# A recurrent attention block and a soft mixture of experts in one kernel: all tasks emitted in another order

## Chip, cores and metric

The kernel runs on one core of a Trainium2 chip. The metric is the device time of one execution in microseconds (us); the figure for the kernel before is the median of three runs. Engines: PE multiplies and transposes (TensorE), DVE, ACT and POOL work elementwise (VectorE, ScalarE, GpSimd), SP issues plain transfers; 16 DMA engines move data.

## What is computed

First a linear recurrence over 768 time steps for 4 batches and 8 heads of width 48, then a soft mixture of 8 experts with 4 slots each over the 3072 rows that come out of it:

```python
for t in range(S):
    kt, vt, rt = (k[:, :, t], v[:, :, t], r[:, :, t])
    cur = np.einsum('bhd,bhe->bhde', u[None] * kt, vt)
    y[:, :, t] = np.einsum('bhd,bhde->bhe', rt, state + cur)
    state = w[None, :, :, None] * state + np.einsum('bhd,bhe->bhde', kt, vt)
...
logits = x @ phi
d = softmax(logits, axis=0); c = softmax(logits, axis=1)
slot_input = (d.T @ x).reshape(E, S_per_e, D)
for e in range(E):
    slot_out[e] = np.maximum(slot_input[e] @ w1[e], 0.0) @ w2[e]
return c @ slot_out
```

(The two softmax lines are shortened; x is y with the heads side by side, 384 wide.) Inputs are float32: r, k, v of 4.7 MB each, w1 and w2 of 12.6 MB each. The output is 3072 x 384 in float32, 4.7 MB.

## The kernel before

**Data.** Time is cut into chunks of 128 steps and blocks of 256. Two batches are handled side by side, so there are 6 blocks U (0 to 5) and 12 steps n of the recurrence (0 to 11; n = 2U and 2U + 1 belong to block U; the state starts anew at n = 6). Loads bring float32 from memory and turn it into bf16 on the way; such loads are issued by POOL. For each block there are six of them, the two halves (batches) of k, r and v in this order: `raw` tile 6U + 2 x which + half, called raw 0 to raw 35 below. Raw 0 alone is loaded by SP and turned by ACT, so raw n is the n-th load on POOL as long as they are in this order. Weights come as one load for each expert (768 KB as bf16): w1 into `w1_all`, w2 into `raw` tiles that are no longer needed; w2 of expert 7 in three parts.

**Work.** `turned` transposes raw tiles on PE (line 419, 16 to a piece), and DVE or ACT writes them to SBUF with the decay factors (lines 430, 427); for blocks after the first, POOL multiplies k by r for each step (line 443, "the product of step n"). `step(n)` transposes k and v back (457), multiplies k by r under a mask (484, 489), forms the sum of k times v and adds the old state (515, 519; the result is `Ssp`), copies it (ACT, 526) and scales it by the decay on POOL (529): this is Z(n, hh), the state behind step n, for the two halves hh of the heads. The next step needs both halves on PE. From the product of line 443 PE and DVE make `dv` (503, 535). The output of a step (552, 557, 559) goes to `x_all`, is transposed (581) and gives the logits (600). `combine` and `dispatch` are the two softmaxes (616 to 652 and 704 to 773; the E sum of line 620 and Le of 636 are on POOL). `first_layer` and `second_layer` are the experts (842 to 905), `output` the last product and the stores (926 to 935, 8 DMAs on SP).

**Order.** Each piece is registered with `task(...)`: engine, assumed duration, what it reads and writes, which buffers it uses. `Plan.order` gives each task a time; when the list `SEQ` is given, it takes the tasks in that order and only computes times. For a load it assumes a queue, and through `lag` that a load waits for the landing of the load `lag` places before it. `Plan.emit` then emits all tasks in that order; where it thinks PE idle at the beginning or after the last step, it puts in filling matmuls (`idle`, line 912). So in this kernel the assumed durations and lags change nothing but the fillers (and which buffer of a ring a task gets); the list is the order.

Every instruction is emitted through `O`, which pins it behind the last instruction emitted on its engine:

```python
def O(ins):
    return tc.keep_in_program_order(ins)
```

A scheduler behind that orders each engine's instructions as pins and data allow. One operation breaks the chain: `pool.affine_select` emits two instructions, a register move (the fill value) and the select. The select is pinned behind the register move, which is itself pinned to nothing. A select, and what is emitted behind it on POOL, is therefore free to move ahead of what was emitted before it. There are four selects of this kind outside the beginning, which build the small matrix `sumI` (lines 679 to 682, tasks 105 to 108 in the numbering of the kernel before):

```python
for i in range(4):
    task(10, "POOL", 0.28, lambda i=i: O(pool.affine_select(
        out=sumI[:], in_=sumI[:], compare_op=ALU.not_equal, fill=1.0, base=-32 * i, ...
```

In the built program each load on POOL takes one of eight semaphores in turn, and waits before its issue for the load that had the semaphore last, the one eight places ahead on POOL.

Of the kernel before, what the change touches and what calls it, by code (L numbers as in the profile page):

```python
# [12 lines left out]
class Plan:  # L13
# [40 lines left out]
    def order(self):  # L54
# [4 lines left out]
            for d in x[4]:  # L59
                after.setdefault(d, []).append(i)  # L60
        ready = [i for i in range(len(tasks)) if not wait[i]]
        t, queue, out = 0.0, 0.0, []
        count, block = 67, -10.0
        while ready:
            best = None
            if self.seq:
                i = self.seq[len(out)]
                assert not wait[i]
                eng, use = tasks[i][1], tasks[i][5]
                at = max(since[i], free.get(eng, 0.0))  # L70
                need = [k[0] for k in use if k not in self.slot]
                for k in need:
                    got = sorted(f for f in self.pools[k] if f is not None)
                    at = max(at, got[need.count(k) - 1])
                best = (at, 0.0, i, at)
            for i in () if self.seq else ready:
                prio, eng, _, _, _, use, _, _ = tasks[i]
                at = max(since[i], free.get(eng, 0.0), t)
                more, hold = self.tune.get(i, (0.0, 0.0))
                if best is not None and at + hold > best[0]:  # L80
                    continue
                need = {}
                for k in use:
                    if k not in self.slot:
                        need[k[0]] = need.get(k[0], 0) + 1
                for k, m in need.items():
                    got = sorted(f for f in self.pools[k] if f is not None)
                    at = max(at, got[m - 1]) if len(got) >= m else 1e9
                key = (at + hold, prio + more, i, at)
                if best is None or key < best:  # L90
                    best = key
            assert best[0] < 1e8, [tasks[i][:3] for i in sorted(ready)[:20]]
            _, _, i, t = best
            prio, eng, dur, fn, deps, use, dma, n = tasks[i]
            for k in use:
                if k not in self.slot:
                    p = self.pools[k[0]]
                    s = min((x for x in range(len(p)) if p[x] is not None), key=lambda x: p[x])
                    self.slot[k] = s
                    p[s] = None  # L100
            if eng == "PE":
                if (count + 2 * n) // 256 > count // 256:

                    part = dur * (256 - count % 256) / (2 * n)
                    begin = max(t + part, block + 6.0)
                    dur += begin - t - part
                    block = begin
                count += 2 * n
            free[eng] = t + dur
            e = t + dur  # L110
            if dma is not None:
                queue = max(queue, t + dur + 1.3) + dma
                e = queue + 1.6
            end[i] = e
            ready.remove(i)
            for d in after.get(i, ()):
                wait[d] -= 1
                since[d] = max(since[d], e + (SAME[eng] if eng == tasks[d][1] and dma is None else LAT[eng]))
                if not wait[d]:
                    ready.append(d)  # L120
            for k in use:
                left[k].discard(i)
                if not left[k]:
                    self.pools[k[0]][self.slot[k]] = max(end[j] + LAT[tasks[j][1]] for j in self.users[k])
            out.append((t, len(out), i))
# [4 lines left out]
    def emit(self, where, fill, took=0.22):  # L130
# [9 lines left out]
            self.tasks[i][3]()  # L140

TUNE = {}
SEQ = [89, 58, 4, 57, 9, 52, 2, 62, 102, 0, 5, 10, 53, 54, 6, 12, 11, 13, 63, 104, 1, 65, 66, 3, 14, 75, 47, 59, 46,
# [27 lines left out]

# [3 lines left out]
def kernel(  # L175
# [32 lines left out]
    f32 = mybir.dt.float32  # L208
# [6 lines left out]
    def O(ins):  # L215
        return tc.keep_in_program_order(ins)

    pe, dve, act, pool, sp = nc.tensor, nc.vector, nc.scalar, nc.gpsimd, nc.sync
# [4 lines left out]
    def sb(name, shape, dt):  # L223
        return big.tile(shape, dt, name=name)
# [56 lines left out]
    ident = sb("ident", [128, 128], bf)  # L281
    by_head = sb("by_head", [128, 128], bf)
    by_time = sb("by_time", [128, 128], bf)
    ones_f = sb("ones_f", [32, 128], f32)
    mask = sb("mask", [128, 128], f32)
    biasP = sb("biasP", [128, 1], f32)
    wuT = sb("wuT", [128, 16], f32)
# [7 lines left out]
    def load(U, which):  # L295
        src = (k, r, v)[which]
        p, n = divmod(U, nU)
        for x in range(2):
# [6 lines left out]
                task(-95, "ACT", 0.83, lambda: O(act.copy(raw_of(0, 0, 0), st)), r=["st"], w=[("raw", 0)])  # L305
            else:
                task(-100 + U, "POOL", 0.54, lambda ap=ap, x=x: O(pool.dma_start(out=raw_of(which, U, x), in_=ap)), w=[("raw", i)],  # L307
                     dma=0.955, lag=7)

    O(act.preload_act_table_set("natural_log_exp_and_others"))  # L310
    both = lambda m: m[:, None, :].to_broadcast([H, 2, D])
# [30 lines left out]
        out=er, in0=Rf, scalar1=-float(C), scalar2=None, op0=ALU.add)), r=["Rf"], w=["er"])  # L342
    for a, b, val in ((0, 128, -200.0), (0, D, 0.0), (64, 64 + D, 0.0)):
        task(-160, "DVE", 0.1, lambda a=a, b=b, val=val: O(dve.memset(biasP[a:b, :], val)), w=["biasP"])
    task(-150, "DVE", 0.1, lambda: O(dve.memset(ones_f[:], 1.0)), w=["ones_f"])
    task(-150, "DVE", 0.1, lambda: O(dve.memset(ucol[:], 0.0)), w=["ucol"])
    for i in range(2):
        task(-150, "DVE", 0.25, lambda i=i: O(dve.memset(Le_t[i][:], 0.0)), w=["Le0"])
# [468 lines left out]
    w2_first = {}  # L817

    def load_w(e, second, part=0):
        lag = 7 if not second and e < 3 else 5  # L820
        if not second:
            task(-50 + e, "POOL", 0.57, lambda: O(pool.dma_start(
                out=w1_all[:, e, :, :], in_=moe_w1[e].rearrange("(p mo) f -> p mo f", p=128))), w=[("w1", e)], dma=3.7, lag=lag)
# [166 lines left out]
```

## Time and profile before

| | |
|---|---|
| three runs | 121.63, 118.66, 119.14 us; median 119.14 |
| the profiled execution | 120.11 us, its span (first to last instruction) 118.3 us |
| PE busy | 99.1 us (84%) |
| DVE, ACT, POOL busy | 92.1, 78.8, 72.5 us |
| software DMA queue (all POOL loads) | 19.47 MB written, 85.7% of 16 engines' time |
| mean granted clock of PE | 0.959 |

Times inside the profile count from the first instruction. The profile has the busy share of each engine in 40 slices and, on demand, in stages; the chain of waits, followed back from the last instruction; the instructions of an engine in order of time, with the idle time ahead of each and what ended it in brackets; and the DMA issues with the median time from issue to landing. A DMA share over 1 comes from packets that overlap.

### The profile page before, as it was taken

To read this page: it belongs to the slowest core of one execution; us is meant where nothing else is said; L and a number is where in the kernel's file an instruction comes from. 1 tells how busy PE (TensorE), PEld (TensorE's weight loads), DVE (VectorE), ACT (ScalarE), POOL (GpSimd) and SP (SyncE) were. 2 spreads that over 40 slices of the span, in tenths; PEclk is the share of its full clock that TensorE was granted. 3 is DMA by queue.
4 is the path that set the end of the run, shared out by engine and by line. 5 is a ranking of instruction groups with operands and counts; after the bars stand their busy time and mean duration, and the time that the engine had idled before them with its cause. 6 is when DMAs were issued, how large, how long until landed. Compare 5 with 4: busy or idle time off the path is not lost.

```text
span 118.3 us, 4300 instructions
## 1 busy us (share of the span) xinstructions
PE 99.1 (84%) x1849; PEld 73.1 (62%) x1849; DVE 92.1 (78%) x156; ACT 78.8 (67%) x161; POOL 72.5 (61%) x112
## 2 busy tenths in 40 slices
PE   4999992999999999999959899989999997656100
PEld 0365781888787788887848687868664554445000
DVE  5999899469999999999979999999976540277400
ACT  4483894299675899899739688978984631265400
POOL 6967768979979988999187878895622300000000
PEclk9999998599999999999999999999999999999955
DMA  2999999999999999999999999999999995069993
GB/s 35 237 189 197 209 206 208 205 208 207 206 200 186 168 208 210 220 211 218 213 220 209 222 209 216 217 212 219 208 219 214 209 206 91 9 224 404 417 415 137
DMA packets 9283, 24.91 MB, mean 210 GB/s; under 512 B 1200, under 2 KB 6192, under 8 KB 9264
## 3 DMA queue, kind: packets, MB, share of 16 engines
q0 software_dynamic: 7632, 19.47, 85.7%
q1 hardware_dynamic: 1584, 5.16, 11.5%
q8 instruction: 14, 0.23, 0.7%
q14 instruction: 5, 0.04, 0.1%
q10 hardware_dynamic: 48, 0.01, 0.0%
HBM read 39.38 MB, written 4.72 MB: 373 GB/s over the span
## 4 chain that ended last, share of the span: by engine, by line
PE 55%; DMA 21%; POOL 5%; issue 4%; DVE 4%; ACT 3%; DVEq 0%; POOLq 0%
PE T L419 12%; DMA raw<-in_moe_w_dram 11%; DMA raw<-in_k_dram 7%; PE T L457 7%; PE Ab L484 6%; PE Y L552 5%; PE T L581 4%; DMA raw<-in_r_dram 4%; PE Y L559 3%; PE Y L515 3%; DVE arena L933 3%; PE Y L557 3%; PE Y L519 3%; POOL raw L307 2%; PE Sb L503 2%
## 5 line engine op out<-in xcount | busy, mean ns | idle before, releaser
L430 DVE TENSOR_TENSOR arena<-T,tab 128x1024 bf16<-128x1024 bf16 x24 | 28.6, 1210 | 3.6 <-PE T L419 3.6
L489 DVE TENSOR_TENSOR arena<-Ab,mask 128x1024 bf16<-128x1024 f32 x24 | 29.2, 1216 | 0.6 <-PE Ab L484 0.5
L419 PE MATMUL T<-by_head,raw 128*48 128x128 bf16 x576 | 22.2, 223 | 0.4 <-issue 0.4
L443 POOL TENSOR_TENSOR arena<-arena 128x1024 bf16<-128x1024 bf16 x10 | 21.4, 2142 | 0.8 <-DVE arena L430 0.8
L529 POOL TENSOR_TENSOR Z<-Ss,wCm 128x384 bf16<-128x384 f32 x20 | 16.6, 833 | 7.6 <-ACT Ss L526 7.5
L419 PEld LDWEIGHTS <-raw 128*48 128x48 bf16 x576 | 17.1, 104 | 4.7 <-issue 2.3
L427 ACT COPY arena<-T 128x1024 bf16<-128x1024 bf16 x12 | 12.1, 1019 | 3.4 <-PE T L419 3.2
L526 ACT COPY Ss<-Y 128x384 f32<-128x384 f32 x20 | 9.6, 491 | 6.3 <-PE Y L519 6.1
L566 ACT CAST x_all<-Y 128x384 bf16<-128x384 f32 x23 | 11.2, 486 | 3.8 <-PE Y L559 3.5
L457 PE MATMUL T<-ident,arena 112*128 112x112 bf16 x176 | 12.4, 217 | 0.0
L535 DVE TENSOR_TENSOR dv<-vn,Sb 128x768 bf16<-128x768 bf16 x12 | 11.3, 943 | 0.4 <-PE Sb L503 0.4
L457 PEld LDWEIGHTS <-arena 112*128 112x128 bf16 x176 | 9.8, 99 | 1.4 <-issue 0.2
L461 ACT COPY vn<-T 128x768 bf16<-128x768 bf16 x12 | 9.7, 810 | 1.1 <-PE T L457 1.1
L584 ACT COPY xT<-T 128x768 bf16<-128x768 bf16 (+1 forms) x12 | 9.1, 790 | 0.9 <-PE T L581 0.9
L484 PE MATMUL Ab<-arena 48*128 48x128 bf16 x192 | 9.5, 219 | 0.0
L519 PEld LDWEIGHTS <-kn 128*128 128x128 bf16 x80 | 5.5, 100 | 5.9 <-issue 4.5
L552 PE MATMUL Y<-vn,arena 128*128 128x48 bf16 x192 | 9.0, 185 | 0.0
L515 PE MATMUL Y<-Z,ident 128*128 128x384 bf16 x16 | 5.5, 345 | 3.9 <-POOL Z L529 3.4
L461 ACT COPY kn<-T 128x768 bf16<-128x768 bf16 x10 | 8.1, 811 | 0.2 <-PE T L457 0.2
L559 PE MATMUL Y<-dv,ident 128*128 128x384 bf16 x24 | 8.0, 333 | 0.0
L307 POOL DMA_DIRECT2D raw<-in_k_dram x11 | 6.0, 551 | 2.6 <-DMA raw<-in_v_dram 1.3
L636 POOL TENSOR_TENSOR Le<-E,rs 128x128 bf16<-128x128 f32 x6 | 2.4, 398 | 8.4 <-ACT tab L853 4.0
(159 smaller groups left out, 204.5 us busy)
## 6 DMA issues: line engine op xcount, KB each, us to landing
w_all<-in_moe_w_dram POOLq DMA_DIRECT2D x8, 768.0 KB, 12.9
raw<-in_moe_w_dram POOLq DMA_DIRECT2D x7, 768.0 KB, 14.5
out_dram<-arena SPq DMA_DIRECT2D x4, 768.0 KB, 5.4
raw<-in_r_dram POOLq DMA_DIRECT2D x12, 192.0 KB, 7.0
raw<-in_v_dram POOLq DMA_DIRECT2D x12, 192.0 KB, 7.0
raw<-in_k_dram POOLq DMA_DIRECT2D x11, 192.0 KB, 6.9
out_dram<-arena SPq DMA_DIRECT2D x3, 192.0 KB, 2.0
out_dram<-arena SPq DMA_DIRECT2D x1, 576.0 KB, 4.0
```

What stands on the lines that cost most here:

```text
L419: O(pe.transpose(T[64 * x:64 * x + D, C * j:C * j + C], raw_of(which, U, x)[:, jj * D:(jj + 1) * D], by_head[:]))
L427: O(act.copy(dst, src))
L430: O(dve.tensor_mul(dst.rearrange("p j (h c) q -> p j h c q", c=2), src.rearrange("p j (h c) q -> p j h c q", c=2), tb[:, :, :, None, :].to ...
L443: O((pool if U else dve).tensor_mul(pr_t[P["pr", 2 * U + b]].rearrange("p (h a) -> p h a", h=H), kt, rt))
L457: O(pe.transpose(T[:, h * C:h * C + 64 + D], cell(st[P[src, U]], h, cc)[0:64 + D], ident[0:64 + D, 0:64 + D]))
L461: O(act.copy(nt[P[name, n]][:].rearrange("p h x d -> p (h x) d")[:, :, 0:D], T[:].rearrange("p (a d) -> p a d", d=64)[:, :, 0:D]))
L484: O(pe.matmul(Ab[:, x, i * C:(i + 1) * C], cell(kt, 4 * rd + i, cc)[s], cell(rt, 4 * rd + i, cc)[s], start=True, stop=True))
L489: O(dve.tensor_mul(AT[:, :, 4 * rd:4 * rd + 4, :], Ab[:].rearrange("p x (h t) -> p x h t", h=4), mask[:, None, None, :].to_broadcast([128, ...
L529: task(n + 0.2 + 0.05 * hh, "POOL", 0.8, lambda hh=hh: O(pool.tensor_mul(Z_t[P["Z", (n, hh)]][:], Ss_t[P["Ss", (n, hh)]][:], wCm[:, 4 * hh ...
L535: O(eng.tensor_mul(dv_t[P["dv", n]][:].rearrange("p h x d -> p (h x) d"), vn_t[P["vn", n]][:].rearrange("p h x d -> p (h x) d"), sums[:, : ...
L552: O(pe.matmul(Y[:, (2 * i + x) * D:(2 * i + x + 1) * D], AT[:, x, h, :], vn[:, h, x, :], start=(i == 0 and x == 0), stop=False, skip_group ...
L559: O(pe.matmul(Y[:, 0:8 * D], ident[:], dv[:, 4 * hh:4 * hh + 4].rearrange("p h x d -> p (h x d)"), start=False, stop=True, skip_group_chec ...
```

## The change

The planner assumes a landing up to 1.8 us later and a lag of 8 instead of 7; the task that set the constant `ones_f` is gone, so every task number from 55 on is one lower; and `SEQ` is another permutation of the 615 tasks that are left.

```diff
@@ order
-        t, queue, out = 0.0, 0.0, []
+        t, queue, loads, out = 0.0, 0.0, 0, []
...
-                e = queue + 1.6
+                e = queue + 1.6 + min(1.8, 0.15 * loads)
+                loads += 1
@@ SEQ
-SEQ = [89, 58, 4, 57, 9, 52, 2, 62, 102, 0, 5, 10, 53, 54, 6, 12, 11, 13, 63, 104, 1, 65, 66, 3, 14, 75, 47, 59, 46,
...
-       80, 19, 97, 20, 78, 21, 22, 90, 92, 91, 23, 81, 24, 93, 25, 105, 26, 27, 106, 98, 48, 116, 28, 83, 87, 113,
...
-       221, 201, 222, 206, 209, 207, 223, 103, 130, 202, 224, 210, 127, 107, 208, 137, 139, 128, 212, 138, 203, 230,
...
-       253, 37, 237, 251, 38, 108, 142, 240, 218, 238, 144, 271, 39, 165, 145, 40, 272, 260, 257, 166, 252, 219, 147,
...
+SEQ = [52, 2, 4, 65, 9, 57, 101, 53, 59, 0, 66, 5, 10, 6, 12, 11, 13, 61, 62, 3, 55, 63, 103, 88, 54, 56, 64, 74, 75,
...
+       267, 159, 333, 318, 301, 161, 302, 490, 282, 300, 307, 178, 304, 334, 179, 288, 319, 335, 305, 322, 310, 104,
+       473, 474, 320, 491, 323, 180, 168, 308, 475, 162, 492, 493, 321, 311, 289, 105, 303, 181, 169, 494, 290, 338,
+       495, 309, 291, 339, 324, 496, 358, 106, 306, 325, 359, 326, 340, 520, 327, 347, 476, 497, 521, 498, 312, 360,
+       313, 361, 356, 163, 499, 344, 174, 345, 357, 314, 350, 351, 477, 328, 315, 341, 336, 342, 329, 522, 175, 500,
+       346, 501, 107, 343, 364, 382, 170, 383, 502, 368, 503, 337, 369, 523, 371, 172, 372, 171, 362, 348, 173, 373,
...
@@ kernel
-    ones_f = sb("ones_f", [32, 128], f32)
...
-                     dma=0.955, lag=7)
+                     dma=0.955, lag=8)
...
-    task(-150, "DVE", 0.1, lambda: O(dve.memset(ones_f[:], 1.0)), w=["ones_f"])
...
-        lag = 7 if not second and e < 3 else 5
+        lag = 8 if not second and e < 3 else 5
```

The selects of `sumI` are tasks 104 to 107 in the new numbering; the loads of w1 for experts 3, 4 and 5 are 473 to 475. The built programs can be compared instruction by instruction. On PE, ACT, DVE and SP both have the order of their list. On POOL neither has. Before, the list has the selects behind raw 15, raw 17, raw 18 and raw 28; in the built program the fourth, with raw 29, 30 and 31 behind it, stands beside the third, ahead of Z(0,0). After, the list has the first select behind Z(3,1), followed on POOL by w1 of experts 3, 4 and 5; in the built program it reads (loads by number, the rest in brackets):

```
raw 1 ... raw 10, [ucol, by_time], raw 11, raw 12, [wCm x2], raw 13, [sumI], w1 expert 3, w1 expert 4, [phi4],
raw 14, [ucol], raw 15, [phi4], raw 16, raw 17, raw 18, [Z(0,0)], raw 19, raw 20, w1 expert 5, [Z(0,1)], raw 21,
raw 22, [Z(1,0)], raw 23, [Z(1,1)], raw 24, raw 25, raw 26, [product 2], raw 27 ... raw 32, [product 3],
raw 33, raw 34, raw 35, [Z(2,0)], w1 expert 0, [Z(2,1)], w1 expert 1, [products 4 and 5], [Z(3,0)], [sumI x3],
[E sum 0], w1 expert 2, [Z(3,1)], [product 6], [Z(4,0)], [Z(4,1)], w1 expert 6, ..., w2 expert 2, [E sum 2],
[product 9], [Z(8,0)], [Z(8,1)], [Z(9,0)], [product 10], w2 expert 3, [Z(9,1)], [product 11], w2 expert 4, ...
```

The filling matmuls of `idle` are 30 instead of 22. Before the first product of step 0 there are 11 instead of 9, behind the last step 19 instead of 13, three of these ahead of the last product of `second_layer`, where there were none.

46 rows, old and new, of the table SEQ are left out of this document.

## The prediction

> **What bounds the kernel now.** I read the slices first, then the stages, then the chain of waits, then POOL in order of time.
>
> ```profile
> span 118.3 us, 4300 instructions
> PEclk9999998599999999999999999999999999999955
> DMA  2999999999999999999999999999999995069993
> ```
>
> The DMA engines are full from about 3 to 98 us, idle around 100, and write the output at the end. The stages (busy us of each engine, granted clock, share of the 16 DMA engines, GB/s) say the same of PE:
>
> ```profile
> 0.00:3.00 3.00, 1.46 (x3) 0.28 (x3) 1.63 (x13) 1.28 (x1) 1.87 (x9) 1.00 0.26 38
> 15.00:18.00 3.00, 2.90 (x78) 2.51 (x73) 3.00 (x4) 3.00 (x6) 2.05 (x6) 1.00 1.16 206
> 18.00:21.00 3.00, 0.99 (x11) 0.68 (x12) 2.51 (x3) 1.18 (x3) 2.58 (x5) 0.82 1.16 208
> 21.00:24.00 3.00, 3.00 (x48) 2.33 (x44) 1.22 (x1) 1.05 (x3) 2.98 (x5) 0.61 1.16 206
> 57.00:60.00 3.00, 2.25 (x52) 1.84 (x49) 3.00 (x4) 1.56 (x5) 0.82 (x1) 1.00 1.04 214
> 60.00:63.00 3.00, 2.49 (x60) 2.22 (x60) 2.09 (x4) 1.91 (x5) 2.96 (x3) 1.00 1.06 219
> 66.00:69.00 3.00, 2.56 (x62) 2.11 (x59) 2.81 (x4) 1.91 (x4) 1.80 (x2) 1.00 1.06 219
> 96.00:99.00 3.00, 2.53 (x61) 1.73 (x56) 0.42 (x1) 0.37 (x1) 0.00 (x0) 1.00 0.97 183
> 99.00:102.00 3.00, 1.96 (x29) 1.34 (x18) 0.00 (x0) 0.58 (x1) 0.00 (x0) 1.00 0.16 27
> ```
>
> So two resources are nearly full at once: the loads, and PE, whose one large hole is at 18 to 21. Whatever stops PE for long is paid, once it exceeds what the last load leaves free. The chain shows who made the hole (start, us, what), and how the loads end:
>
> ```profile
> 10.41 7.89 DMA raw<-in_k_dram
> 18.30 0.28 issue
> 18.59 0.52 POOL raw L307
> 19.11 0.86 POOL Z L529
> 20.01 0.48 PE Y L515
> ...
> 88.96 12.55 DMA raw<-in_moe_w_dram
> ...
> 101.54 0.88 PE Y L891 x8
> ```
>
> A load issued at 10.41 landed at 18.30; POOL, held up behind it, issued the next load, then made Z, and only then could PE go on at 20.01. POOL issues all loads and also makes Z (line 529) and the products of line 443, strictly in order: a load that must wait holds up the recurrence. That is the place to look at in the changed program. POOL around it, and where the kernel later stands:
>
> ```profile
> 7.17 0.52 POOL L307 DMA_DIRECT2D raw<-in_v_dram  x1 [0.33 <-DMA raw<-in_r_dram]
> 14.21 0.51 POOL L307 DMA_DIRECT2D raw<-in_v_dram  x1 [0.45 <-DMA raw<-in_r_dram]
> 16.15 0.51 POOL L307 DMA_DIRECT2D raw<-in_k_dram  x1 [0.86 <-DMA raw<-in_v_dram]
> 16.66 0.50 POOL L680 TENSOR_SCALAR_AFFINE_SELECT sumI<-sumI 128x32 f32<-128x32 f32 x2
> 18.59 0.52 POOL L307 DMA_DIRECT2D raw<-in_k_dram  x1 [0.37 <-DMA raw<-in_k_dram]
> 21.01 0.84 POOL L529 TENSOR_TENSOR Z<-Ss,wCm 128x384 bf16<-128x384 f32 x1
> 27.32 2.18 POOL L443 TENSOR_TENSOR arena<-arena 128x1024 bf16<-128x1024 bf16 x1
> 30.46 2.16 POOL L443 TENSOR_TENSOR arena<-arena 128x1024 bf16<-128x1024 bf16 x1
> 34.94 0.83 POOL L529 TENSOR_TENSOR Z<-Ss,wCm 128x384 bf16<-128x384 f32 x1 [0.81 <-ACT Ss L526]
> 37.05 1.16 POOL L822 DMA_DIRECT2D w_all<-in_moe_w_dram  x2
> 41.29 0.41 POOL L620 TENSOR_TENSOR E<-Lall,rm 128x128 f32<-128x128 f32 x1
> 45.26 2.13 POOL L443 TENSOR_TENSOR arena<-arena 128x1024 bf16<-128x1024 bf16 x1
> 75.34 0.82 POOL L529 TENSOR_TENSOR Z<-Ss,wCm 128x384 bf16<-128x384 f32 x1
> 94.01 0.58 POOL L829 DMA_DIRECT2D raw<-in_moe_w_dram  x1
> ```
>
> The load at 18.59 is the 21st on POOL and waited for the 13th (the one that landed at 18.30). So already before the change a load waits for the landing of the load eight places ahead, as both built programs have it. The planner's lag of 7 or 8 is only its assumption; "eight in flight" changes nothing on the chip by itself.
>
> **The change part by part.** The order on PE, ACT, DVE and SP is the listed one. On POOL it is not. The first sumI select now stands far down the list, followed there by three loads of w1 (experts 3, 4, 5), and since the selects break the chain of pins, select and loads float forward in the built program: two of these loads directly behind raw 13 (the second half of k of block 2, the 13th load on POOL), ahead of all r and v of block 2; the third behind raw 20 (half of r of block 3) and ahead of Z(0,1). Sizes and landings:
>
> ```profile
> w_all<-in_moe_w_dram POOLq DMA_DIRECT2D x8, 768.0 KB, 12.9
> raw<-in_v_dram POOLq DMA_DIRECT2D x12, 192.0 KB, 7.0
> ```
>
> A raw load is 196,608 bytes: 0.95 us at 206 GB/s (15 to 18 us). A weight load is 786,432: 3.67 us at 214 (57 to 60). Transfers are taken in the order of issue, as the row at 18.59 suggests. Up to raw 13 nothing changes on the queue, so it lands at 18.30. The two weight loads land at 21.97 and 25.64; the raw loads 14 to 20 follow at 26.6, 27.5, 28.5, 29.5, 30.4, 31.4, 32.3; the third weight load at 36.0; raw 21 to 24 at 36.9, 37.9, 38.8, 39.8.
>
> POOL now, with 0.29 us from a landing to the issue (18.30 to 18.59), 0.54 for a raw issue, 0.58 for a weight issue and the durations above. Z(0,0) comes about 0.9 earlier, since no load that waits for raw 13 is ahead of it any more. Raw 20, eight places behind the first weight load, waits until 22.3. The third weight load waits for the second, 25.93, and is out at 26.5. Only then Z(0,1): 26.5 to 27.35, where it ran from 21.01. Behind it raw 21 and 22, Z(1,0), raw 23, Z(1,1), raw 24 to 26, each a little ahead of POOL or level with it, then the product of step 2 from 32.25 to 34.4 (it began at 27.32). Raw 28 waits for the third weight load, 36.3; raw 29 to 32 wait for raw 21 to 24, 37.2, 38.2, 39.1, 40.1; so the product of step 3 runs from 40.6 to 42.75 (it began at 30.46). Three raw issues to 44.4, Z(2,0) to 45.2 (it began at 34.94), a weight issue, Z(2,1) and another to 47.2. The products of steps 4 and 5 to 51.5, Z(3,0) to 52.3, the three other selects (0.25 each) and the E sum (0.41) to 53.5, a weight issue, and Z(3,1) to 54.9. The set of POOL work up to there, product of step 5 included, was done before at 45.26 + 2.13 = 47.4: **+7.5**.
>
> Does PE pay that? The recurrence needs each Z and the dv of each step, and PE stands in order behind them. At Z(0,1) alone: PE restarts after Z(0,0) at about 19.1 (20.01 less 0.9) and has three pieces ahead of the next wait (a round of Y, two transposes of v). From rows of such pieces,
>
> ```profile
> 25.45 0.56 PE T L419 x16
> ...
> 28.16 0.31 PE Y L552 x8
> 28.47 0.17 PE Y L557 x4
> ...
> 84.32 0.75 PE Ab L912 x3
> ```
>
> two at 0.56, and 0.5 plus a closing matmul for the Y, with 0.5 for the Ssp round: until about 21.4. It then stands for 27.4 - 21.4 = 6 us, where before it stood 2.1 (17.9 to 20.0). The rest of the 7.5 comes at the product of step 3 and Z(2,0). PE was full from 24 to 57, so nothing there takes the delay back; I take 7.5 whole.
>
> The clock: the hole at 18 was followed by 0.82 and 0.61 of the clock, that is (0.18 + 0.39) x 3 / 0.5 = 3.4 us at half speed, at most 1.7 lost. The 6 us hole will bring the same once more, in place of the old fall: 0 net, and part of it hides behind the wait for the product of step 3. By the row, a hole of 2.1 us was enough, so the later waits at 43 to 45 can add a second fall: 1.7, kept for the upper end. By the Trainium skill, "TensorE: Matmul & The Clock Gate", Part 1, half speed follows an idle window of about 3.4 us; by that only the 6 us hole counts, and the sum stays as it is. This trace agrees with the length of the window (3.4 at half speed), not with the need for a whole idle one (2.1 was enough).
>
> The end: the wait of PE for the last loads goes, if the loads are ahead of PE.
>
> ```profile
> PE Y L891 <- DMA raw<-in_moe_w_dram: 1.0, 2, 0.6
> ```
>
> That is -1.0. The load of w2 for expert 3 now stands behind the product of step 10 and Z(9,0), which ended at 76.2; 7.5 later it is issued at about 83.7, with data near 85.5 (the issue at 37.05 showed its data about 2 us on). With five weight loads, 18.4 us, still to come out of a queue that was busy until 99, the queue would be empty at 80.6, so it stands idle for some 5 us and ends at 103.9; before, the last landing (101.5) came 2.5 after the queue emptied, so now at 106.4. PE needs it at 101.54 - 0.6 + 7.5 = 108.4: ahead by 2. The last part of w2, issued at 94.01 behind the E work of block 5, moves to about 101.3, still before the queue ends.
>
> The plan also emits 30 instead of 22 filling matmuls (line 912). Three of them stand in front of the last product: 3 x 0.25 = +0.75 (0 if PE waits there); the other changes lie in waits. The missing memset is one of 13 DVE instructions that filled 1.63 of the first 3 us, 0.13 at most and hidden by the wait for the first k; without that cover it is a gain of 0.13. The rest of the new order (which piece of PE work goes before which) moves waits that nothing in this trace prices: besides the hole, PE lost 0.75 at 57 to 60, 0.51 at 60 to 63 and 0.44 at 66 to 69, so the order can give back some 1.7 us or add as much; I take 0.
>
> Sum: 7.5 - 1.0 + 0.75 = +7.25. The profiled execution took 120.11 with a span of 118.3; it becomes 127.4 with a span of 125.6. The median of the three runs is 119.14, 0.97 below the profiled one: **126.4**.
>
> **Rivals.** *The loads set the end, the delay is absorbed* (the other side). The bytes and the queue are the same; if PE arrived at its last product within the 1.0 us it waits now, the end would stay. It decides below a delay of 1 us, which needs POOL to reach Z(0,1) by about 22, so the weight loads must not hold up raw 20. For it: DMA is full nearly everywhere. Against: a load that waits for the eighth ahead is in the rows. This gives 118.1 to 120: 0.06.
>
> *The built order is not what runs, or loads share the engines instead of following each other*: then the listed order stands, the hole at 18 shrinks or goes, and with the loads still ending near 101.5 at most the 1.0 at the end and part of the tail are won: 116 to 119, of which I give 0.02 to under 116.7 and count the rest with the first rival. Against: POOL's rows of before already show such a float (the selects at 16.66 side by side, loads of a later block behind them).
>
> *Starved weights*: the idle queue of 5 us grows by over 2, the last load falls behind PE, and each us that POOL is later at expert 3 of w2 is a us at the end. It decides once that load is issued after 86. With 2 to 4 us of this and a second fall of the clock (1.7): 130 to 132, given 0.08.
>
> **How the numbers follow.** The forecast has 0.84, its own range runs from +4.8 (1.7 given back by the order, 0.75 of fillers free) to +10.6 (1.7 added, and the second fall of 1.7): 123.9 to 129.8. The range is 123.0 to 130.0: the lower end leaves room for hand-made landings that are 0.9 late in all, the upper end touches the third rival, and the two cases that are left out on either side hold 0.16. What can be told from no change is about 2%, 2.4 us. Faster 0.02; within 0.06; slower 0.92, the forecast and the third rival.
>
> **What would show it.** On POOL two w_all issues at 11 to 13 and one near 26, Z(0,1) near 26.5 instead of 21.0, the product of step 3 near 40.6; a hole in PE from 21 to 27 and half clock behind it; DMA below 0.9 somewhere in 80 to 86; PE no longer waiting for w2 at line 891. I am wrong if Z(0,1) runs before 23, if the w_all issues all stand after 34, or if PE's hole closes without the end moving.

## The result and the profile after

| | before | after |
|---|---|---|
| median, us | 119.94 (118.66 to 121.63, 4 runs) | 126.98 (126.78 to 129.85, 4 runs) |
| ratio after to before | | 1.067, 95% interval 1.062 to 1.073 |
| span of the profiled execution, us | 118.3 | 125.2 |

The changed kernel is slower by 6.7%. Medians here are over all runs; ratios leave out runs more than 1.5% above the fastest of the same kernel. A second set of six runs of it, beside the last experiments, gave 126.33 (126.03 to 127.09) and 1.065 (1.059 to 1.071).

The page of the changed kernel, first line and slices:

```profile
span 125.2 us, 4321 instructions
PE   4999997009999969978999999999999999865200
PEclk9999999965799999999999999999999999999955
DMA  2999999999999999999959999909999993049993
```

A slice is 3.1 us. PE has two slices of 0 (21.9 to 28.2), where before it had one slice of 2 (17.7 to 20.7). The queue of loads, full nearly to the end before, now has a dip in slice 21, a nearly empty slice 27 and, as before, a gap near the end. The stages of the changed kernel (start and end, length, busy us and count of PE, PEld, DVE, ACT and POOL, granted clock, DMA share, GB/s):

```profile
21.00:24.00 3.00, 0.26 (x10) 0.19 (x5) 1.91 (x2) 1.41 (x3) 0.51 (x1) 1.00 1.05 217
24.00:27.00 3.00, 0.00 (x0) 0.00 (x0) 0.00 (x0) 0.00 (x0) 0.47 (x1) 0.87 1.08 196
27.00:30.00 3.00, 1.99 (x29) 1.81 (x28) 0.22 (x1) 0.89 (x2) 2.98 (x6) 0.50 1.16 207
30.00:33.00 3.00, 3.00 (x46) 2.30 (x42) 2.36 (x3) 1.19 (x2) 2.93 (x6) 0.50 1.17 228
...
63.00:66.00 3.00, 3.00 (x72) 2.56 (x69) 3.00 (x6) 3.00 (x9) 2.98 (x3) 1.00 0.73 126
66.00:69.00 3.00, 3.00 (x73) 2.37 (x71) 3.00 (x5) 2.43 (x5) 2.71 (x6) 1.00 0.81 154
...
81.00:84.00 3.00, 3.00 (x68) 2.24 (x66) 2.81 (x5) 2.39 (x5) 2.98 (x4) 1.00 0.15 30
84.00:87.00 3.00, 3.00 (x68) 2.38 (x67) 3.00 (x5) 2.65 (x6) 3.00 (x3) 1.00 0.78 131
```

From 24 to 27 nothing at all computes; POOL waits, and begins to issue one load. Half clock follows for (0.13 + 0.50 + 0.50) x 3 / 0.5 = 6.8 us. POOL in order of time shows why (start, length in us, line, operation, and in brackets the idle time ahead of it and what ended it):

```profile
11.63 0.58 POOL L821 DMA_DIRECT2D w_all<-in_moe_w_dram  x1 [0.19 <-issue]
12.60 0.53 POOL L821 DMA_DIRECT2D w_all<-in_moe_w_dram  x1 [0.40 <-DMA raw<-in_k_dram]
...
23.47 0.51 POOL L307 DMA_DIRECT2D raw<-in_r_dram  x1 [4.02 <-DMA w_all<-in_moe_w_dram]
...
26.53 0.56 POOL L821 DMA_DIRECT2D w_all<-in_moe_w_dram  x1 [2.55 <-DMA w_all<-in_moe_w_dram]
27.11 0.84 POOL L528 TENSOR_TENSOR Z<-Ss,wCm 128x384 bf16<-128x384 f32 x1
...
36.85 0.51 POOL L307 DMA_DIRECT2D raw<-in_v_dram  x1 [1.48 <-DMA w_all<-in_moe_w_dram]
...
41.17 2.14 POOL L442 TENSOR_TENSOR arena<-arena 128x1024 bf16<-128x1024 bf16 x1
...
44.81 0.88 POOL L528 TENSOR_TENSOR Z<-Ss,wCm 128x384 bf16<-128x384 f32 x1
...
54.25 0.84 POOL L528 TENSOR_TENSOR Z<-Ss,wCm 128x384 bf16<-128x384 f32 x1
```

The two early w1 loads go out at 11.63 and 12.60. Raw 20 waits 4.0 us for the first of them, the third w1 load 2.6 for the second, raw 28 1.5 for the third; Z(0,1) stands behind the first two of these waits and starts at 27.11, the product of step 3 behind all of them at 41.17. The waits of the whole run (us in total, times, longest) and the chain:

```profile
PE Y L514 <- POOL Z L528: 8.4, 3, 6.7
POOL raw L307 <- DMA w_all<-in_moe_w_dram: 5.5, 2, 4.0
POOL w_all L821 <- DMA w_all<-in_moe_w_dram: 2.6, 1, 2.6
```

```profile
12.60 13.64 DMA w_all<-in_moe_w_dram
...
27.11 0.84 POOL Z L528
...
31.09 9.27 DMA raw<-in_k_dram
...
41.17 2.15 POOL arena L442
```

The first 43 us of the chain are loads and POOL. There is no wait of PE for the loads of w2 left at the end; PE's own work is last there.

### The profile page after: what moved, and what is told of

The parts are those of the page before. It is cut to its first block, busy times and chain, and to the rows that moved or that the text cites. A ratio compares the mean times of both kernels' runs of the same rounds, so it can differ in the third digit from the quotient of the medians.

```text
span 125.2 us, 4321 instructions
## 1 busy us (share of the span) xinstructions
PE 102.6 (82%) x1857; PEld 75.4 (60%) x1857; DVE 92.7 (74%) x155; ACT 79.2 (63%) x161; POOL 72.8 (58%) x112
## 4 chain that ended last, share of the span: by engine, by line
PE 45%; DMA 24%; POOL 14%; DVE 5%; ACT 3%; issue 2%; DVEq 0%; POOLq 0%
DMA raw<-in_k_dram 13%; DMA w_all<-in_moe_w_dram 11%; PE T L418 7%; POOL Z L528 5%; PE T L456 4%; POOL raw L307 4%; PE Ab L911 4%; PE Ab L483 4%; POOL arena L442 3%; PE Y L551 3%; DVE arena L932 3%; PE T L580 3%; PE Y L558 2%; PE Y L514 2%; PE Y L556 2%
## 5 line engine op out<-in xcount | busy, mean ns | idle before, releaser
L418 PE MATMUL T<-by_head,raw 128*48 128x128 bf16 x576 | 23.5, 231 | 0.1
L418 PEld LDWEIGHTS <-raw 128*48 128x48 bf16 x576 | 18.0, 108 | 4.5 <-issue 2.0
L456 PE MATMUL T<-ident,arena 112*128 112x112 bf16 x176 | 12.9, 220 | 0.0
L307 POOL DMA_DIRECT2D raw<-in_r_dram x12 | 6.5, 547 | 4.7 <-DMA w_all<-in_moe_w_dram 4.0
L307 POOL DMA_DIRECT2D raw<-in_v_dram x12 | 6.3, 530 | 3.1 <-DMA w_all<-in_moe_w_dram 1.5
```

Of the source, the lines that this page charges most:

```text
L418: O(pe.transpose(T[64 * x:64 * x + D, C * j:C * j + C], raw_of(which, U, x)[:, jj * D:(jj + 1) * D], by_head[:]))
L456: O(pe.transpose(T[:, h * C:h * C + 64 + D], cell(st[P[src, U]], h, cc)[0:64 + D], ident[0:64 + D, 0:64 + D]))
```

## The experiments

The theory: three w1 loads that floated to the front hold POOL up, and PE stands behind POOL. Rivals: the list itself is worse, whatever POOL does; the planner's constants; the clock; the data that come late, rather than POOL.

**The list as written.** Each instruction is also pinned behind the instruction that was emitted last on its engine, so that the selects and the loads behind them can't float. Done once with the list of the changed kernel and once with that of the kernel before:

```diff
     def O(ins):
-        return tc.keep_in_program_order(ins)
+        ins = tc.keep_in_program_order(ins)
+        e = ins.ins.engine
+        if e in behind:
+            tc.add_manual_dep(ins.ins, behind[e], ...)
+        behind[e] = ins.ins.name
+        return ins
```

> The changed kernel with every select also pinned to the instruction ahead of its register move, so POOL runs the listed order and the three w1 loads stand behind Z(3,1). Theory (the early weight loads make the loss): the hole in PE at 21 to 27 is gone, Z(0,1) begins near 20, the end is set by the loads again: 117.5 to 120 us, ratio 0.98 to 1.01 to the kernel before. Rival (the new order of the work on PE, ACT and DVE, or the fillers, costs a good part): still 123 us or more, ratio 1.03 or more.

> The kernel before with the selects pinned, so raw 29 to 31 go back behind raw 28 as listed. Control for the two above. Theory: Z(0,0) begins near 18 instead of 19.1 and the hole in PE shrinks from 2.1 to about 1 us, but the loads still set the end: 118 to 120 us, ratio 0.98 to 1.0. Rival (raw 29 to 31 early is what keeps the queue full later): ratio over 1.01.

With the list of after: 117.52 us, ratio to the kernel before 0.985 (0.979 to 0.992). With the list of before: 117.68, ratio 0.987 (0.980 to 0.993), a little under what was expected. POOL with the list of after pinned, Z(0,1) and the product of step 3:

```profile
18.25 0.86 POOL L536 TENSOR_TENSOR Z<-Ss,wCm 128x384 bf16<-128x384 f32 x1
...
29.61 2.14 POOL L450 TENSOR_TENSOR arena<-arena 128x1024 bf16<-128x1024 bf16 x1
```

Both run 9 to 12 us earlier than in the changed kernel. PE has no hole (from 3 to 96 us no stage of 3 us has it busy for less than 2.38), and the granted clock stays at 1.00 up to 108. So the new list is not worse than the old; what is worse is what the built program makes of it. The rival that the list itself costs the time falls. The kernel before had a float of its own (its fourth select, with raw 29 to 31 behind it, ahead of Z(0,0)) and paid 1.8 us for it. Both pinned kernels beat it, by less than 2%. With the list of before pinned, the last load sets the end, landing at 98.8:

```profile
86.32 12.47 DMA raw<-in_moe_w_dram
```

With the list of after pinned, the chain at that time is PE's own: it works on its last fillers from 98.43 and on the last product from 99.03.

**The loads moved in the old list.** In the kernel before, w1 of experts 3 and 4 are listed behind raw 13 and that of expert 5 behind raw 20, and the lag that the planner assumes for these loads is set aside; the rest of the list is the old one:

```diff
-... 91, 23, 81, 24, ... 229, 30 ...
+... 91, 23, 474, 475, 81, 24, ... 30, 476, ...
```

> The kernel before with nothing but w1 of experts 3 and 4 listed behind raw 13 and of expert 5 behind raw 20 (their lag in the planner set aside). Theory: the same loss without the new order: 124.5 to 128 us, ratio 1.04 to 1.07, Z(0,1) near 27. Rival: under 121.5 us, ratio under 1.02.

123.31 us, ratio 1.036 (1.028 to 1.044): slower as expected, but 1.2 under the lower end. With the selects listed behind the loads here, no load floats past them in the built program, so its control is the pinned kernel before: 117.68, and the moved loads cost 5.6. Its longest wait is that of after; another, for late data of v, is new:

```profile
PE Y L514 <- POOL Z L528: 8.1, 3, 6.4
PE T L418 <- DMA raw<-in_v_dram: 1.7, 2, 0.9
```

```profile
36.00:39.00 3.00, 1.33 (x29) 0.93 (x27) 2.50 (x3) 1.23 (x2) 1.86 (x5) 1.00 1.16 209
...
45.00:48.00 3.00, 3.00 (x74) 2.45 (x72) 3.00 (x5) 2.03 (x5) 3.00 (x4) 1.00 1.16 208
```

Three loads in a list that is otherwise the old one make the same hole. They cost less than in the new list, and why was not isolated: at 45 to 48 PE is full here, where in the changed kernel it lost 0.74, but at 36 to 39 it lost 1.67 to the late v, where the changed kernel lost nothing.

**The constants alone.** The kernel before with the planner's landing times and lags of after (which gives it four more fillers):

```diff
-                e = queue + 1.6
+                e = queue + 1.6 + min(1.8, 0.15 * loads)
+                loads += 1
...
-                     dma=0.955, lag=7)
+                     dma=0.955, lag=8)
```

> The kernel before with the planner's new constants alone (later landings, lag 8), its list unchanged; only the number of fillers changes. Theory: a load waits for the eighth ahead in both, so the planner's lag does nothing on the chip: within 0.7 us of the kernel before, ratio 0.994 to 1.006. Rival (one more load in flight helps): ratio 0.99 or less.

119.62 us, ratio 1.002 (0.998 to 1.006). No effect of theirs can be told; it is within 0.6%.

**Two loads, or the third alone.** From the pinned list of after, either experts 3 and 4 behind raw 13, or expert 5 behind raw 20 (in both the planner's lag for these loads is set aside):

```diff
-... 91, 23, 97, ...
+... 91, 23, 473, 474, 97, ...
```

```diff
-... 203, 30, 229, ...
+... 203, 30, 475, 229, ...
```

> The pinned changed kernel (117.5 us) with w1 of experts 3 and 4 listed behind raw 13, expert 5 left behind Z(3,1). Theory (POOL stands at the load eight places behind each early weight load): raw 20 waits to 22.3, raw 21 to 25.9; Z(0,1) near 22.8 and Z(1,0) near 27; no third wait before the product of step 3, so about 4 to 6 us of the 9.5: 121.5 to 123.5 us. Rival (the third load is what decides, since Z(0,1) stands right behind it): under 120 us.

> The pinned changed kernel with only w1 of expert 5 listed behind raw 20. Theory: raw 20 and the weight load itself wait for raw loads that have landed, so Z(0,1) stays near 20.5; raw 28 waits for its landing near 29, later loads land 3.7 later: 0.5 to 2.5 us, 118 to 120 us. Rival: 122 us or more.

Two early: 121.51 (121.22 to 122.6), ratio 1.016 (1.012 to 1.021), 4.0 more than pinned. The third alone: 118.81 (117.35 to 119.75), ratio 0.991 (0.987 to 0.996), 1.3 more; here the interval overlaps that of the pinned kernel (0.979 to 0.992), so these 1.3 are not clear of noise. POOL with two early:

```profile
22.08 0.51 POOL L314 DMA_DIRECT2D raw<-in_r_dram  x1 [2.77 <-DMA w_all<-in_moe_w_dram]
22.60 0.84 POOL L535 TENSOR_TENSOR Z<-Ss,wCm 128x384 bf16<-128x384 f32 x1
```

and with the third alone:

```profile
18.20 0.58 POOL L829 DMA_DIRECT2D w_all<-in_moe_w_dram  x1 [0.20 <-issue]
...
28.83 0.51 POOL L315 DMA_DIRECT2D raw<-in_v_dram  x1 [1.47 <-DMA w_all<-in_moe_w_dram]
```

With two, raw 20 waits for the first as in after and Z(0,1) follows at 22.60. The third, when it is alone, goes out at 18.20 without waiting, in front of the same Z. In the changed kernel it waits for the second until 26.53. So the three do not add (4.0 + 1.3 against 8.8 to 9.5 for all three). The rest, 3.5 to 4.2, comes only with all three early, when the third stands behind the second, ahead of Z(0,1); that this wait is the reason is read from the rows, not tested alone.

**The clock.** 26 matmuls on a zeroed tile in PE's hole, ahead of the second half of the sum of step 1, to keep the clock up:

```diff
+                for _ in range(26 if (n, hh) == (1, 1) else 0):
+                    O(pe.matmul(Y[:, 0:512], warm[:, 0:128], warm[:, 0:512], start=True, stop=True))
```

> The changed kernel with 26 matmuls of zeros on PE ahead of the second Ssp round of step 1, where it stands from 21 to 28. Theory: the clock stays at 1.00 through 27 to 33, but PE then waits longer for the product of step 3 and Z(2,0), which POOL sets: 0 to 0.8 us less than the changed kernel, ratio 1.055 to 1.075 to the kernel before. Rival (the fall of the clock is paid in full: half speed over 5 us of work): 2 us or more less, ratio 1.05 or less.

Four runs of 126.22, 128.57, 128.78 and 129.01, where the changed kernel takes 126.98. The lowest is 0.76 less, inside what the theory gave; the others are longer; the rival's 2 us less is in none. No ratio can be given from these. The stages are those of the run of 128.57:

```profile
42.00:45.00 3.00, 1.23 (x32) 1.11 (x33) 2.42 (x5) 1.02 (x2) 3.00 (x4) 1.00 1.16 211
45.00:48.00 3.00, 2.03 (x23) 1.41 (x20) 0.18 (x1) 2.23 (x4) 2.98 (x5) 0.52 1.15 204
48.00:51.00 3.00, 3.00 (x56) 2.59 (x53) 2.12 (x2) 0.48 (x1) 2.98 (x3) 0.50 1.15 221
```

There the hole is filled (PE is busy throughout 24 to 27) and the clock stays at 1.00 up to 45, but PE then catches up with POOL sooner, stands at 42 to 48 while POOL is full, and the clock falls there instead, for (0.48 + 0.50 + 0.16 in the next stage) x 3 / 0.5 = 6.8 us. This shows that the fall could be moved, not what one costs.

**The fillers at the end.** The changed kernel without the three filling matmuls ahead of the last product, run twice, the second time beside the changed kernel itself; and the pinned one without them:

```diff
-    P.emit(lambda i: warmed <= i and ... or P.spans[i][0] > P.spans[y_done][0], idle)
+    last = P.writers["SOl", 0] + P.writers["SOl", 1]
+    P.emit(lambda i: i not in last and (warmed <= i and ... or P.spans[i][0] > P.spans[y_done][0]), idle)
```

> The changed kernel without the three fillers ahead of the last product of the second layer; they do nothing for the output. Theory: the last load landed before them, so they are paid in full, 0.75 us: 126.0 to 126.5 us where the changed kernel has 127.0. Rival (PE would wait there anyway): 126.8 to 127.2 us.

> The changed kernel once more, to have it beside the same kernel without its last fillers on one chip. Theory: 126.5 to 127.5, ratio about 1.065.

> The changed kernel without the three filling matmuls ahead of the last product (which are left out). Theory (they cost their own busy time, 0.75, since the last load lies ahead of PE): 0.5 to 1.0 us less than the changed kernel of the same job; the rest of the 1.35 seen before was the phase of the clock. Rival (taking them out also shifts the clock): 1.3 us less or more.

> The changed list with POOL pinned to it, and without the filling matmuls ahead of the last product. Theory (here the last load sets the end and covers them): 117.1 to 117.6, no difference from the pinned kernel's 117.5. Rival (they cost here as well): 0.75 less, 116.8 or below.

The first time 125.63 (124.86 to 127.04), 1.35 under the changed kernel's 126.98, more than their busy time. Side by side: 126.33 (126.03 to 127.09) with them, 125.68 (125.37 to 126.49) without, 0.65 less; the ratios to the kernel before, 1.065 (1.059 to 1.071) and 1.059 (1.054 to 1.064), overlap, so the runs alone do not settle the size. The chains do. With the fillers:

```profile
107.11 0.75 PE Ab L911 x3
...
108.58 0.42 ACT so L902
```

Without, the chain goes from the last pieces of line 884 on PE over line 901 on ACT to line 902, which starts at 107.61:

```profile
106.81 0.16 PE Sb L884 x3
...
107.00 0.58 ACT so L901
...
107.61 0.41 ACT so L902
```

That is 0.97 earlier, of which 0.13 had been won ahead of the tail: 0.84 for the fillers. In the pinned kernel their removal does nothing: 117.91 (117.38 to 119.52, 12 runs) against 117.52, ratios 0.991 (0.987 to 0.995) and 0.985 (0.979 to 0.992). There the last load covers them; without them it is what the last product waits for, landing at 98.8, where with the fillers that product began at 99.03:

```profile
83.92 14.89 DMA raw<-in_moe_w_dram
```

**POOL's own work first.** The pinned list of after with all three w1 loads as far ahead of the raw loads as the changed kernel has them, but with POOL's Z and products listed ahead of the loads that would wait:

```diff
-raw 19, raw 20, w1 5, Z(0,1), raw 21, raw 22, Z(1,0), raw 23, Z(1,1), ..., product 2, raw 27 ... raw 32, product 3
+Z(0,0), Z(0,1), Z(1,0), Z(1,1), products 2 and 3, raw 19, raw 20, w1 5, raw 21 ... raw 26, Z(2,0), Z(2,1),
+products 4 and 5, raw 27 ... raw 31, Z(3,0), raw 32 ... raw 35, ...
```

> The changed list with POOL pinned, and the three w1 loads as far ahead of the raw loads as the changed kernel has them, but POOL's own Z and products listed ahead of every load that would wait (raw 19 and later ones behind the products). The raw data of blocks 3 to 5 then comes later still. Theory (the loss is POOL standing behind a load's wait while its own work is ready): 117.5 to 120. Rival (the loss is the late data itself, so PE starves whatever POOL does): 122 or more.

123.82 us (123.42 to 125.58), ratio 1.042 (1.034 to 1.049): the rival's side, so the theory as it was put here, that POOL alone makes the loss, missed. PE's wait for Z is gone (0.4 us in all), but another has come:

```profile
PE T L425 <- DMA raw<-in_v_dram: 6.7, 4, 3.8
PE Y L521 <- POOL Z L535: 0.4, 1, 0.4
```

PE in order of time, where it waits:

```profile
28.95 0.24 PE L425 MATMUL T<-by_head,raw 128*48 128x128 bf16 x1 [1.57 <-DMA raw<-in_v_dram]
29.86 1.07 PE L425 MATMUL T<-by_head,raw 128*48 128x128 bf16 x31 [0.68 <-DMA raw<-in_v_dram]
...
40.78 0.30 PE L425 MATMUL T<-by_head,raw 128*48 128x128 bf16 x1 [3.84 <-DMA raw<-in_v_dram]
41.73 1.04 PE L425 MATMUL T<-by_head,raw 128*48 128x128 bf16 x15 [0.65 <-DMA raw<-in_v_dram]
```

POOL is no longer in the way and PE runs almost without a stop from 18 to 27, and then lacks v of block 2 (raw 16 and 17) until 28.95 and 29.86, and v of block 3 (raw 22 and 23) until 40.78 and 41.73. The first pair stands on the queue where the changed kernel has it, behind two weight loads; the prediction worked out 28.5 and 29.5 for its landing. That wait, 2.3 us, is a price of the early loads themselves. The second pair is later here than in the changed kernel, since its issue stands behind POOL's products; there they landed at about 38.5 and 39.4 (by the issues at 38.74 and 39.71 that waited for them, less the 0.29 from a landing to an issue), so PE, which wanted them here at 36.94, would have waited until about 39.4 instead of 41.73, an estimate of 2.2 in place of 4.5. So freeing POOL alone gives back 2.5 of the 8.4 us that lie between 126.33 and the 117.91 of the same comparison (pinned, without the last fillers), and would give back some 4.8, an estimate, if the raw loads were no later than in the changed kernel. That version was not tried.

## Why the prediction was right, and where not

**The float and the semaphore wait** were the cause, as argued. The list without the float takes 117.5, the three loads moved by hand in the old list cost 5.6, and every wait of the sum is in POOL's rows. The third w1 load: let go at 25.93 and out at 26.5 in the forecast, 26.53 and 27.09 measured, since the second landed 0.6 later than reckoned. So Z(0,1): 26.5 against 27.11. Raw 20 was let go at 23.47 instead of 22.3, with no effect, because the third load's wait came after it. Product of step 3: 40.6 against 41.17. Z(3,1) done: 54.9 against 55.1. The third weight load came 0.6 later than reckoned (let go at 36.85 for 36.3).

**The 7.5 us taken whole** held: POOL is 7.7 later at Z(3,1), and the span is 125.2 against 125.6 forecast. The terms as measured, 7.7 - 1.0 + 0.84 for the fillers, make 7.5; the span grew by 6.9. Where the other 0.6 came back was not isolated. The median, 126.98 against 126.4 forecast, lies 7.0 above that of the kernel before in the same comparison. But the step had one thing missing: POOL was taken as the only way in which the early loads reach PE. The last experiment shows a second, the late v of blocks 2 and 3, right behind it, and the loads moved in the old list had already lost 1.7 to it. It changed no number in the changed kernel, where PE came late enough to find its data; it would have spoilt a forecast for the repair.

**The clock** was mis-sized: one fall of 3.4 us was reckoned for the 6 us hole, in place of the old one, and 6.8 came. The forecast of no net cost was near enough all the same, because PE, slow or not, had to wait for POOL again, as the prediction said of a part of it: 0.23 for the product of step 3, until 43.37, and 0.96 for Z(2,0):

```profile
45.74 0.32 PE L514 MATMUL Y<-Z,ident 128*128 128x384 bf16 x1 [0.96 <-POOL Z L528]
```

The half speed lies at 24 to 33. From 12.6 to 43.3 the chain holds only loads and POOL, and no row of POOL in that time waits for PE after 24, so in this trace the 6.8 us held up nothing that the end depends on. In the kernel before, PE's slow work from 20.0 on stands on the chain. So a fall that was paid was replaced by a longer one that was not; whether this is the 0.6 above is not shown.

**The end.** PE no longer waits for w2 at line 890 (891 before), -1.0 as forecast, and the three fillers cost 0.84 in the trace and 0.65 in the medians for the 0.75 reckoned. The idle stretch of the queue is there: at 81 to 87 it moved 30 and 131 GB/s of the 219 of its full stages, (189 + 88) x 3 / 219 = 3.8 us for the forecast 5. The load that ends it was issued at 83.30, for 83.7 forecast. Not foreseen was the thinner stretch at 63 to 69, (93 + 65) x 3 / 219 = 2.2 us: with three weight loads taken from the middle of the queue to its front, it runs dry there as well. The two together make 6.0, and the last load still came ahead of PE.

**The rest at 0**: the constants at 0 (ratio 1.002) and the other order at 0 (pinned, the two lists are at 0.985 and 0.987). The memset was not tried alone.

**The rivals.** That the loads set the end and absorb the delay did not happen in the changed kernel; in the pinned kernel before, and in the pinned one without the last fillers, the last load does set the end. The listed order, given 116 to 119, takes 117.5 when it really runs, so the built order was the thing to read. The weights did not starve PE: expert 3 of w2 went out 2.7 before the point of 86.

## What to carry to other kernels

An order that is written out is only as good as the pins that hold it: where one operation is emitted as two instructions, look at the built order of the engine that issues loads before judging the list, since here the list as written takes 1.5% less than the kernel before, and what was built from it 6.7% more. On an engine that both issues loads and computes, price a load by what it must wait for and by the work that stands behind it, and pull a large load forward only past small loads whose data nobody needs soon. When such a wait is removed, ask at once which data were late behind it, because the engine it fed will stand there next.

## What the runs showed of the hardware

In these traces half speed of PE comes in pieces of about 3.4 us. Summed over the stages up to 100 us, (1 - clock) x 3 / 0.5, it lasted 3.4 us in the kernel before and in the one with the constants alone, 3.4 twice with two loads early (at 24 to 30 and at 33 to 39), and 6.8 in the changed kernel (both traces), in its second run without the last fillers, with the third load alone, in the loads moved in the old list, in the filled hole and with POOL's own work first. In the first run without the last fillers it was 10.3:

```profile
24.00:27.00 3.00, 0.00 (x0) 0.00 (x0) 0.00 (x0) 0.00 (x0) 1.32 (x2) 0.57 1.13 202
27.00:30.00 3.00, 2.87 (x43) 2.48 (x44) 0.95 (x1) 1.28 (x2) 2.99 (x6) 0.50 1.15 206
30.00:33.00 3.00, 3.00 (x46) 2.29 (x43) 2.50 (x3) 0.80 (x1) 3.00 (x5) 0.50 1.12 225
33.00:36.00 3.00, 3.00 (x54) 2.32 (x52) 1.08 (x2) 1.76 (x3) 1.46 (x3) 0.72 1.06 201
```

(0.43 + 0.50 + 0.50 + 0.28) x 3 / 0.5 = 10.3 after a hole of 6.3 us, where the changed kernel's hole of 6.7 gave 6.8: the number of pieces does not follow the hole alone. The Trainium skill, "TensorE: Matmul & The Clock Gate", Part 1, has a free-running window of 3413 ns, and multiples of it are what the traces show. It asks for a whole idle window before the fall; here a hole of 2.1 us in the kernel before, and of 1.7 with the constants alone, was enough. And the most half speed did not make the slowest run: the kernel with 10.3 had a span of 123.1, the same kernel with 6.8 one of 123.6.
